# Loads of units 8 to 11 on GpSimd's queue, unit 11 finished by itself, and a new static order

## The chip, the cores and the metric

The kernel runs on one core of one Trainium2 chip. The metric is device time in microseconds (us) of one execution, median of the runs shown. The engines are TensorE (PE, with its weight loads PEld), VectorE (DVE), ScalarE (ACT), GpSimd (POOL) and SyncE (SP). SP does no arithmetic here; it issues DMAs, and so does POOL.

## The reference, cut to what matters

```python
# q, k, v: (8, 8, 576, 64) float32: batch, head, position, head_dim
scores = q @ k.transpose(0, 1, 3, 2) / sqrt(64)
gamma = 1 - 2.0 ** (-5 - arange(8))                  # one per head
D = where(i >= j, gamma ** (i - j), 0)               # i, j: positions
x = ((scores * D) @ v).transpose(0, 2, 1, 3).reshape(4608, 512)
h = x @ w_in                                         # (512, 2048)
g = maximum(0.01 * h, h)
out = g @ w_out                                      # (4608, 512) float32
```

This is a retention layer (causal, with a decay per head and no softmax) and behind it a feed-forward layer with a leaky ReLU.

## The kernel before

**Units.** The 4608 tokens are 36 units of 128 tokens (two chunks of 64), and 9 groups of 512 tokens (four units each). Jobs are named in the code after what they do, and this text uses those names; `u` is a unit, `g` a group.

**Retention, one unit at a time.** `ld{u}.{1,0,2}` loads k, q and v of a unit in float32 (L504; three DMAs, six where the unit spans two batches). `ck{u}` casts k to float16 on ACT (L528), `cq{u}` and `cv{u}` multiply q and v by decay tables (L531, L534; from unit 8 on they are POOL's). `tr{u}` transposes q and k by a DMA that SP issues (L544); units 0 to 7 are transposed on TensorE instead (`tp`, L560, copied out by `yt`, L565). `sa` and `sb` are 16 small matmuls each: the scores of the two chunks (L590) and the new states, k times v (L599). `mk{u}` masks the scores (L605, DVE), `st{u}.{j}` carries the running state from chunk to chunk (L656 to L661, DVE), `sx{u}` casts the states to float16 (L675 or L678, POOL or ACT by the planner's choice). Then the outputs: masked scores times v, and states times q (L697). `x{u}` copies them to the tile xT, the input of the feed-forward layer (L748).

From unit 9 on these matmuls come in bursts: `bu{u}` does, in one job, the rest of the outputs of unit u-2, the first part of the outputs of unit u-1, and `sa` and `sb` of unit u. All bursts share one PSUM tile for outputs (`shared`). A last job `oz` finishes units 34 and 35. So the outputs of unit 11 are complete after bu13.

**Feed-forward.** `h{g}.{f0}.{t0}` are plain blocks of the first product (L822): in groups 0 and 1 four 128-row blocks of w_in for 128 tokens (16 matmuls of 128 columns), from group 2 on one block for 512 tokens (four matmuls of 512 columns). From group 2 on half of the first product is done in two sets of seven smaller products (Strassen's scheme with Winograd's sums): `s{g}.{i}.{1..7}`, four matmuls of 256 columns each (L907), with sums of inputs `xs` (L884) and of weights `ws` (L864), and additions on DVE (L930). `l...` applies the leaky ReLU (L828, L942, ACT). The second product is a set of seven for each group: `p{g}.{1..7}`, 16 matmuls of 256 columns each (L1078), with sums `m{g}` on DVE (L1052), of weights `wm` (L1014), with copies and additions `k1`, `u2`, `v` (L1092, L1094; `k11` is the copy for group 1) and outputs `y` (L1112, L1114). `so{g}.{a}` stores half a group (L1025, SP).

**Weights.** `wi0` to `wi3` load w_in, `wo0` to `wo3` load w_out, both on POOL's queue (L796, L803). Idle stretches of TensorE at the start are filled with matmuls on zeros (`fill`, L1173).

**What sets the order.** The kernel is written out by a planner. Every job gets an engine (or a choice of engines), a cost, the jobs that it comes after, the buffers it opens and uses, and a due time. `Plan.order` plays the jobs through once with those costs and takes at each step the job that can begin first, the more urgent one among those within `slack`; the instructions are then issued in that order, each engine's in its own queue, in order. So costs, due times, the assumed time from a transfer's end to its landing (`land`), safety margins (`SAFE`) and the seed of a small random shift of due times all act on one thing, the order (and the choice of engine where there is one). Loads on POOL's queue follow the string `order` in CFG, where a number is a unit; units beyond its last number are SP's. `aheads` says after which unit's loads each transpose may stand on SP's queue. `gate='wo3'` holds SP's first steady job until the last part of w_out has landed. Loaded tiles have five buffers for each of q, k and v, transposed and cast tiles four.

```python
for u in range(8, NU + 9):
    for j in [loaded[u, x] for x in (1, 0, 2)] if u < NU else []:
        if j.eng == "SP":
            steady(j)
    while to_turn and to_turn[0] + (CFG["aheads"] + (CFG["ahead"],) * NU)[to_turn[0] - 8] <= u:
        steady(turned[to_turn.pop(0), 0])
```

Of the kernel before, what the change touches and what calls it, by code (L numbers as in the profile page):

```python
# [10 lines left out]
FP = mybir.dt.float32  # L11
# [36 lines left out]
class Plan:  # L48
# [62 lines left out]
    @staticmethod  # L111
    def land(eng, t):

        if eng == "SP":
            return 800
        return 900 + min(max(0, t - 5000) * 0.13, 2000) if t < 26000 else 1200
# [169 lines left out]

def _cfg(order="1 wi0 wi1 2 3 wi2 wi3 4 5 6 7 wo0 wo1 wo2 wo3", gate="wo1", nsets=2, at=(4, 9, 14, 99), mk=(), st="POOL", **kw):
    nset = {g: nsets for g in range(2, 9)}
# [8 lines left out]
    for g in range(2, 9):  # L297
        n = nset[g]
        rest = [f for f in blocks if not any(f % 8 in (2 * i, 2 * i + 1) for i in range(n))]
        items = [("b", f) for f in rest]  # L300
        for i in range(n):
            items.insert(min(len(items), at[i]), ("s", i))
        main += [("s" if n else "b", g, items if n else rest), ("L2", g, None)]
# [12 lines left out]
    c = dict(  # L316
        sets=sorted(g for g in nset if nset[g]), set_ids=range(max(nset.values())), ws="POOL/DVE", xs="POOL/DVE",
        ws_due=60000, l1="1627534", one=("a", "b"),
        gate=gate, aheads=(), mask16=bool(mk), ld=5, ap=4, main=main, unit=unit, loads=loads, t0=9000, extra=1300, l_late=1000,
        l2="1265734", l2z="1265734", early=0, margin=60, slack=60, fill_until=60000,  # L320
        split=lambda u: u < 4,
        joined=8, safe=(0, 0), ahead=2, seed=0, noise=0, wm=("DVE/POOL",) * 4, mix=lambda g, n: "DVE", keep="ACT", lead=4500, spread=6500,
    )
# [27 lines left out]
    st='POOL/ACT',  # L351
    aheads=(2, 2, 1, 2, 1, 1, 2),
)
# [3 lines left out]
def kernel(  # L357
# [87 lines left out]
    def half(i):  # L445
# [133 lines left out]
    def inner(u, se, me="DVE"):  # L579
# [37 lines left out]

        if u > J0:
            two = u > J0 + 1

            def burst():
                if two:
                    part_of(u - 2)[1](landed[u - 1])
                part_of(u - 1)[0]()
                sa()
                sb()

            before = outer_needs(u - 1) + ([copied[u - 3]] if u > J0 + 2 else [])
            ja = jb = add(
                f"bu{u}", "PE", (640, 840), burst,  # L630
                [turned[u, 0], turned[u, 1], cast[u, 1], cast[u, 2]] + before, [a, shared],
                [qkT[u], qk16[u], v16[u]] + outer_uses(u - 1) + (outer_uses(u - 2) if two else []), mode="q",
            )
# [12 lines left out]
        for j in range(2):  # L646
# [19 lines left out]
            if scaled and before is not None:  # L666
                c = (c[0] + 400, c[1] + 400)
            after = [jb] + ([before[2]] if before else [])
# [95 lines left out]

    J0 = CFG["joined"]
    shared = Buf(ot_pool, [P, 2, 2, NP, CH], FP, "ot", True, turn=J0)
    parts = {}

    def part_of(u):
        if u not in parts:  # L770
            parts[u] = sums(u, shared, u % 2, u % 2)
        return parts[u]

    def finish():
        u = NU - 1

        def run():
            part_of(u - 1)[1](landed[u])
            part_of(u)[0]()
            part_of(u)[1]()  # L780

        j = add(
            "oz", "PE", (800, 1000), run, outer_needs(u) + [copied[u - 2]], [], [shared] + outer_uses(u) + outer_uses(u - 1), mode="q"
        )
        outer_copy(u - 1, j, shared, (u - 1) % 2, (u - 1) % 2)
        outer_copy(u, j, shared, u % 2, u % 2)
# [393 lines left out]
    for what, g, items in CFG["main"]:  # L1180
# [4 lines left out]
        elif what == "s":  # L1185
            T += sum(865 if kind == "b" else 3600 for kind, f in items)
        else:
# [29 lines left out]
    for u in range(NU):  # L1217
# [7 lines left out]
        if u < J0:  # L1225
            outer(u)
    finish()
    what, n = CFG["gate"]
# [17 lines left out]
    for (what, g, items), t in zip(CFG["main"], starts):  # L1246
# [6 lines left out]
        elif what == "s":  # L1253
            sum_x(g, t)
            at = t
            for kind, f in items:
                if kind == "b":
                    layer1(g, f, 1, 0, TOK, at)
                else:
                    layer1_set(g, f, at)  # L1260
                at += 865 if kind == "b" else 3600
        elif what == "b":
# [52 lines left out]
```

## Time and profile before

| | |
|---|---|
| median of 3 runs | 295.06 us (294.38 to 295.63) |
| the profiled execution | 298.08 us, its span 296.3 us |
| granted TensorE clock | 0.988 of full speed in the mean |
| TensorE busy | 280.9 us (95%) |
| DVE, ACT, POOL busy | 213.6, 155.2, 116.5 us |
| DMA | 50.07 MB; SP's queue 37.76 MB, POOL's 11.54 MB |
| loads issued on POOL | ld0.2 (v of unit 0) and all of units 1 to 9, w_in, w_out |
| loads issued on SP | k and q of unit 0, all of units 10 to 35 |

How to read it: the profile is of one execution, and its times are from the start of the span. Each engine works through its instructions in order; a row's bracket gives the idle time before it and what ended that. "Issue" stands for idle time of an engine that waited for nothing the profile shows. A busy TensorE may still be slower than its peak, so stretches are compared by the starts of jobs. Queue 8 carries TensorE's instructions, 35 transfers of 16 KB. Landings of DMAs are taken from the trace's records.

### The profile page before, as it was taken

The page shows a single profiled execution, that of the slowest core. Times are in us where ns is not written, and L with a number is a line of the kernel's source. Part 1 is how long each engine was busy: PE and PEld are TensorE (multiplying, and loading weights), DVE is VectorE, ACT ScalarE, POOL GpSimd, SP SyncE. Part 2 cuts the span into 40 slices and gives each one's busy share as a digit, 9 for nine tenths or more (in the row PEclk, how much of TensorE's full clock was granted, in tenths as well). Part 3 has the DMA queues.
Part 4 walks back from the last instruction along what each step waited for, and adds up shares of the span by engine and source line. Part 5 has one row for each costly group of instructions (what it writes and reads, how often), then busy time and mean ns, then how long its engine had stood idle before and what let it go on. Part 6 is the DMA issues. An engine that isn't in the chain of part 4 may idle for free.

```text
span 296.3 us, 10315 instructions
## 1 busy us (share of the span) xinstructions
PE 280.9 (95%) x4478; PEld 219.8 (74%) x4478; DVE 213.6 (72%) x366; ACT 155.2 (52%) x281; POOL 116.5 (39%) x128
## 2 busy tenths in 40 slices
PE   7989987999999979999999999999999999999994
PEld 3567986888787657867886787678767876786683
DVE  2568574976898578867985897599668876845662
ACT  2576763735334853278338724783486157705710
POOL 8859683803625435743333324335433211000000
PEclk9999998899999997999999999999999999999999
DMA  7999999399999999989989977999996130003003
GB/s 154 286 246 155 290 216 335 90 195 208 230 223 183 234 214 249 213 236 189 187 155 246 168 160 188 215 181 153 270 144 69 38 145 2 2 0 145 0 2 142
DMA packets 125006, 50.07 MB, mean 169 GB/s; under 512 B 114080, under 2 KB 118816, under 8 KB 124960
## 3 DMA queue, kind: packets, MB, share of 16 engines
q1 hardware_dynamic: 118096, 37.76, 62.5%
q0 software_dynamic: 6576, 11.54, 16.8%
q8 instruction: 35, 0.57, 0.9%
q10 hardware_dynamic: 288, 0.11, 0.1%
q14 instruction: 11, 0.09, 0.1%
HBM read 36.81 MB, written 9.44 MB: 156 GB/s over the span
## 4 chain that ended last, share of the span: by engine, by line
PE 77%; DMA 9%; DVE 5%; issue 4%; POOL 2%; SPq 2%; ACT 0%; DVEq 0%; POOLq 0%
PE acc L1078 33%; PE acc L822 23%; PE acc L907 13%; DMA w_in<-in_moe_w_in_dram 5%; PE ot L697 4%; DMA t<-in_q_dram 3%; PE sc L599 2%; PE sc L590 1%; SPq L544 1%; DVE mix L1052 1%; POOL st L675 1%; POOL qk L531 1%; PE acc L560 1%; DVE s L605 1%; DVE v L534 0%
## 5 line engine op out<-in xcount | busy, mean ns | idle before, releaser
L822 PE MATMUL acc<-xT,w_in 128*128 128x128 f16 (+1 forms) x736 | 89.6, 270 | 2.5 <-issue 2.0
L1078 PEld LDWEIGHTS <-gt 128*128 128x128 f16 x720 | 70.5, 99 | 12.2 <-issue 1.7
L828 ACT ACTIVATE gt<-acc 128x512 f16<-128x512 f32 x88 | 51.9, 595 | 34.0 <-PE acc L822 33.2
L822 PEld LDWEIGHTS <-w_in 128*128 128x128 f16 x736 | 51.8, 99 | 19.1 <-issue 3.2
L531 POOL TENSOR_TENSOR qk<-t,cs 128x512 f16<-128x512 f32 x29 | 32.3, 1114 | 58.6 <-DMA t<-in_q_dram 26.1
L1078 PE MATMUL acc<-w_out,gt 128*128 128x256 f16 x432 | 53.8, 280 | 1.4 <-ACT k L1092 1.3
L748 ACT CAST xT<-ot 128x512 f16<-128x512 f32 x35 | 20.4, 586 | 31.8 <-PE ot L697 31.8
L534 POOL TENSOR_TENSOR v<-t,cs 128x512 f16<-128x512 f32 x29 | 33.3, 1149 | 6.4 <-DMA t<-in_v_dram 3.7
L1078 PE MATMUL acc<-w_mix,gt 128*128 128x256 f16 x288 | 34.4, 273 | 0.0
L1078 PEld LDWEIGHTS <-mix 128*128 128x128 f16 x288 | 28.0, 98 | 3.3
L528 ACT CAST qk<-t 128x512 f16<-128x512 f32 x36 | 22.4, 621 | 9.9 <-DMA t<-in_k_dram 9.8
L942 ACT ACTIVATE gt<-sy 128x512 f16<-128x512 f32 x42 | 25.8, 627 | 2.9 <-DVE sy L930 2.2
L907 PEld LDWEIGHTS <-w_in 128*128 128x128 f16 x224 | 21.6, 98 | 7.3
L605 DVE TENSOR_TENSOR s<-sc,cs 128x512 f16<-128x512 f32 x36 | 24.5, 682 | 1.9 <-PE sc L590 1.7
L930 DVE TENSOR_TENSOR sa<-acc,sk 128x512 f32<-128x512 f32 x14 | 9.7, 691 | 18.0 <-PE acc L907 17.5
L907 PEld LDWEIGHTS <-ws 128*128 128x128 f16 x168 | 15.8, 98 | 7.0
L930 DVE TENSOR_TENSOR sy<-acc,sa 128x512 f32<-128x512 f32 x28 | 18.8, 685 | 2.5 <-PE acc L907 1.8
L697 PE MATMUL ot<-qkT,st 64*64 64x64 f16 x512 | 17.0, 198 | 3.3 <-POOL st L675 2.3
L658 DVE TENSOR_TENSOR s<-sc,s 128x256 f32<-128x256 f32 x40 | 16.7, 416 | 3.6 <-PE sc L590 2.2
L697 PEld LDWEIGHTS <-st 64*64 64x64 f16 x512 | 11.4, 107 | 10.5 <-issue 7.5
L1114 DVE TENSOR_TENSOR osb<-acc,u 128x512 f32<-128x512 f32 (+1 forms) x19 | 12.5, 660 | 8.4 <-PE acc L1078 8.4
L1052 DVE TENSOR_TENSOR mix<-gt 128x1024 f16<-128x1024 f16 x18 | 14.2, 819 | 4.6 <-ACT gt L942 4.0
(65 smaller groups left out, 411.6 us busy)
## 6 DMA issues: line engine op xcount, KB each, us to landing
out_dram<-osb SPq DMA_DIRECT2D x17, 512.0 KB, 4.0
t<-in_k_dram SPq DMA_DIRECT2D x24, 256.0 KB, 4.0
t<-in_q_dram SPq DMA_DIRECT2D x24, 256.0 KB, 4.2
t<-in_v_dram SPq DMA_DIRECT2D x23, 256.0 KB, 4.3
t<-in_v_dram POOLq DMA_DIRECT2D x9, 256.0 KB, 7.7
w_in<-in_moe_w_in_dram POOLq DMA_DIRECT2D x8, 256.0 KB, 7.2
t<-in_k_dram POOLq DMA_DIRECT2D x8, 256.0 KB, 8.2
t<-in_q_dram POOLq DMA_DIRECT2D x8, 256.0 KB, 8.2
```

Source lines behind the costliest of these rows:

```text
L528: copies[e](out=t[:, 1], in_=t32[u, 1][:])
L531: engine[e].tensor_tensor(out=t[:, 0], in0=t32[u, 0][:], in1=decay(u, 0), op=MUL)
L534: engine[e].tensor_tensor(out=s[:], in0=t32[u, 2][:], in1=decay(u, 1), op=MUL)
L605: landed[u] = nc.vector.tensor_tensor(out=s[:], in0=a[:, :, 0], in1=mask_sb.unsqueeze(1).unsqueeze(1).to_broadcast([P, 2, NP, CH]), op=MUL,)
L697: i = nc.tensor.matmul(out=o[half(oo), j ^ swap, slot, c, :], lhsT=lhsT, rhs=rhs, start=(j, oo) not in seen, stop=True, skip_group_check=True,
L748: copies[e](out=x_of(u).rearrange("q c (j t) -> q c j t", j=2), in_=i.rearrange("q j c t -> q c j t"))
L822: nc.tensor.matmul(out=a[:, n, :], lhsT=w_in16[:, c, (f0 + n) * P : (f0 + n + 1) * P], rhs=x[:, c, t0 : t0 + nt], start=(c == 0), stop=(c ...
L828: nc.scalar.activation(out=y[:, f0 : f0 + nf, t0 : t0 + nt], in_=a[:], func=mybir.ActivationFunctionType.Lrelu)
L907: nc.tensor.matmul(out=o[:, m, :], lhsT=lhs[:, c, m * P : (m + 1) * P], rhs=rhs[:, c, :], start=fresh and m == 0 and c == 0, stop=c == 1, ...
L930: nc.vector.tensor_tensor(out=z[:], in0=o[:], in1=keeps[to][:], op=ADD)
L942: nc.scalar.activation(out=y[:, f0 : f0 + 2, half_], in_=z[:], func=mybir.ActivationFunctionType.Lrelu)
L1078: nc.tensor.matmul(out=r[:, tb, :], lhsT=lhs()[:, f, tb * P : (tb + 1) * P], rhs=rhs[:, f, :], start=fresh and i == 0, stop=f == HF - 1, s ...
```

## The change

1. **Loads.** Units 10 and 11 go from SP's queue to POOL's, and the order on POOL's queue is written anew: the loads of unit 1 before wi0, unit 5 before wi3, unit 7 before wo2 and wo3. SP has no load between unit 0's and unit 12's; its first steady job, held by the gate, is now tr8.
2. **Unit 11.** The units from 8 on are split in two segments, 8 to 11 and 12 to 35, each with an output tile of its own in turn. A new job `oz11` finishes the outputs of units 10 and 11 together, after p1.7 in the new order; bu12 holds only `sa` and `sb`. `oz` becomes `oz35`.
3. **The planner's picture.** The assumed landing on SP's queue is 1500 ns after the transfer instead of 800, the safety margin behind a transfer 2000 instead of 1000; several costs, due times, `aheads` and the seed differ. Code for half-width blocks (`halves`) is added and not used.

The order that results has, around what the text speaks of:

```
PE before   ... p0.7 bu9 p0.3 p0.4 bu10 p1.1 p1.2 bu11 p1.6 p1.5 bu12 p1.7 p1.3 bu13 p1.4 s2.0.1 ...
            ... s2.1.5 bu15 s2.1.4 h2.7.0 s2.1.3 h2.15.0 p2.1 bu16 p2.2 p2.6 p2.5 p2.7 bu17 p2.3 p2.4 s3.0.1 ...
PE after    ... p0.7 sa8 p0.3 bu9 p0.4 p1.1 bu10 p1.2 p1.6 bu11 p1.5 p1.7 oz11 p1.3 bu12 p1.4 s2.0.1 ...
            ... s2.1.4 s2.1.3 bu14 p2.1 bu15 p2.2 p2.6 bu16 p2.5 p2.7 bu17 p2.3 p2.4 s3.0.1 bu18 ...
POOL before ... ld8 ld9 cq8 cq9 cv8 cq10 cv9 cv10 sx8 cq11 ... cq18 sx15 cv18 ...
POOL after  ... ld8 ld9.1 cq7 cv7 ld9.0 ld9.2 ld10 ld11 cq8 cq9 cv8 cq10 cv9 sx8 cv10 cq11 ... cv22 cq23 sx20 ...
SP before   ld0 ld10 tr8 ld11 tr9 tr10 ld12 ld13 tr11 so0.0 tr12 so0.1 ld14 tr13 ld15 ld16 tr14 ...
SP after    ld0 tr8 tr9 tr10 ld12 tr11 ld13.1 ld13.0 so0.0 so0.1 ld13.2 tr12 ld14 ld15 ld16 tr13 ...
```

The core of the diff:

```diff
         if eng == "SP":
-            return 800
+            return 1500
...
+    ends = sorted(closes) + [35]
+    segs = tuple(zip([joined] + [z + 1 for z in ends[:-1]], ends))
...
 CFG = _cfg(
-    lead=6000,
-    spread=7000,
-    at=(2, 7, 9, 14),
-    l1='1672534',
+    lead=12000,
+    spread=7500,
+    at=(2, 8, 9, 10),
+    l1='1627543',
...
-    slack=60,
-    l_late=500,
-    extra=800,
-    t0=9000,
+    slack=30,
+    l_late=1000,
+    extra=1600,
+    t0=5000,
...
-    seed=211,
+    seed=296,
...
-    safe=(150, 1000),
-    order='wi0 1 2 wi1 3 4 wi2 wi3 5 wo0 6 wo1 wo2 wo3 7 8 9',
+    safe=(150, 2000),
+    order='1 wi0 2 wi1 3 4 wi2 5 wi3 wo0 6 wo1 7 wo2 wo3 8 9 10 11',
...
-    aheads=(2, 2, 1, 2, 1, 1, 2),
+    aheads=(2, 2, 1, 1, 1, 3, 3),
+    lead2=2000,
+    spread2=7000,
+    closes=(11,),
...
-        "f16": dict(ACT=(505, 640), DVE=(370, 460)),
+        "f16": dict(ACT=(490, 640), DVE=(340, 440)),
...
-        "mul": dict(DVE=(620, 740), POOL=(1010, 1090)),
-        "mix": dict(DVE=(700, 860), POOL=(2050, 2150)),
-        "sum": dict(DVE=(370, 470), POOL=(1010, 1100)),
+        "mul": dict(DVE=(605, 740), POOL=(1010, 1090)),
+        "mix": dict(DVE=(610, 780), POOL=(2050, 2150)),
+        "sum": dict(DVE=(340, 450), POOL=(1110, 1200)),
...
-        if u > J0:
-            two = u > J0 + 1
+        first = first_of.get(u)
+        if first is not None and (u > first or first > J0):
+            one, two = u > first, u > first + 1
+            shared = shares[first]

             def burst():
                 if two:
                     part_of(u - 2)[1](landed[u - 1])
-                part_of(u - 1)[0]()
+                if one:
+                    part_of(u - 1)[0]()
                 sa()
                 sb()
...
-    def finish():
-        u = NU - 1
+    def finish(u):
+
+        f = last_of[u]
+        shared = shares[f]
...
     def x_due(u):
-        return first[u // 4] - CFG["lead"] - CFG["spread"] * (3 - u % 4) if u >= 8 else 1e9
+        if u < 8:
+            return 1e9
+        lead, spread = CFG["lead2" if u < 12 else "lead"], CFG["spread2" if u < 12 else "spread"]
+        return first[u // 4] - lead - spread * (3 - u % 4)
...
-    finish()
+        if u in last_of:
+            finish(u)
```

More of the change, by code (lines that the diff above doesn't have):

```diff
@@ L284, in order, with _cfg @@
         return out
-def _cfg(order="1 wi0 wi1 2 3 wi2 wi3 4 5 6 7 wo0 wo1 wo2 wo3", gate="wo1", nsets=2, at=(4, 9, 14, 99), mk=(), st="POOL", **kw):
+def _cfg(order="1 wi0 wi1 2 3 wi2 wi3 4 5 6 7 wo0 wo1 wo2 wo3", gate="wo1", nsets=2, at=(4, 9, 14, 99), mk=(), closes=(11,), joined=8, halves=(), at2=(8, 9, 10, 11), st="POOL", **kw):
     nset = {g: nsets for g in range(2, 9)}
@@ L321, in _cfg @@
         split=lambda u: u < 4,
-        joined=8, safe=(0, 0), ahead=2, seed=0, noise=0, wm=("DVE/POOL",) * 4, mix=lambda g, n: "DVE", keep="ACT", lead=4500, spread=6500,
+        safe=(0, 0), ahead=2, seed=0, noise=0, wm=("DVE/POOL",) * 4, mix=lambda g, n: "DVE", keep="ACT", lead=4500, spread=6500, lead2=6000, spread2=6000,
     )
@@ L623, in burst @@
                     part_of(u - 2)[1](landed[u - 1])
[L624 to L628 removed]
+                if one:
+                    part_of(u - 1)[0]()
+                sa()
+                sb()
+            before = outer_needs(u - 1) if one else []
+            if u > first + 2:
+                before.append(copied[u - 3])
             ja = jb = add(
[L630 to L632 removed]
+                f"bu{u}", "PE", (640, 840) if one else (290, 490), burst,
+                [turned[u, 0], turned[u, 1], cast[u, 1], cast[u, 2]] + before, [a] + ([shared] if one else []),
+                [qkT[u], qk16[u], v16[u]] + (outer_uses(u - 1) if one else []) + (outer_uses(u - 2) if two else []), mode="q",
             )
@@ L763, in outer @@
         outer_copy(u, j, o)
-    J0 = CFG["joined"]
-    shared = Buf(ot_pool, [P, 2, 2, NP, CH], FP, "ot", True, turn=J0)
+    J0 = CFG["segs"][0][0]
+    shares = {f: Buf(ot_pool, [P, 2, 2, NP, CH], FP, "ot", True, turn=J0 + i) for i, (f, _) in enumerate(CFG["segs"])}
+    first_of = {u: f for f, z in CFG["segs"] for u in range(f, z + 1)}
+    last_of = {z: f for f, z in CFG["segs"]}
     parts = {}
@@ L1185 @@
         elif what == "s":
-            T += sum(865 if kind == "b" else 3600 for kind, f in items)
+            T += sum({"b": 865, "h": 890, "s": 3600}[kind] for kind, f in items)
         else:
```

20 lines of the change are left out of this document (14 added, 6 removed).

## The prediction

> **What bounds the kernel now.** The page first: engine shares, and the slices (40 of 7.4 us).
>
> ```profile
> PE 280.9 (95%) x4478; PEld 219.8 (74%) x4478; DVE 213.6 (72%) x366; ACT 155.2 (52%) x281; POOL 116.5 (39%) x128
> ...
> PE   7989987999999979999999999999999999999994
> ...
> PEclk9999998899999997999999999999999999999999
> DMA  7999999399999999989989977999996130003003
> ```
>
> TensorE is the bound: only 15.4 us of the span are not busy, and two slices lie at a lower clock. The chain of waits, in order of time, says from where on nothing can be won (start, length, what):
>
> ```profile
> 139.54 1.75 PE acc L1078 x16
> ...
> 167.94 1.75 PE acc L1078 x16
> ...
> 196.38 1.75 PE acc L1078 x16
> ...
> 224.79 1.75 PE acc L1078 x16
> ```
>
> These are the first products p3.1, p4.1, p5.1 and p6.1. They stand 28.40, 28.44 and 28.41 us apart, all work of TensorE. So a gain must come before 125 us. The timeline around the largest gap there (start, length, engine, line, operation; the bracket is idle time and what ended it):
>
> ```profile
> 109.15 1.39 POOL L531 TENSOR_TENSOR qk<-t,cs 128x512 f16<-128x512 f32 x1 [4.99 <-DMA t<-in_q_dram]
> 110.50 1.07 POOL L675 CAST st<-s 128x512 f16<-128x512 f32 x1
> 111.62 0.26 PE L697 MATMUL ot<-qkT,st 64*64 64x64 f16 x2 [2.31 <-POOL st L675]
> 112.30 3.16 PE L1078 MATMUL acc<-w_out,gt 128*128 128x256 f16 x16
> 115.29 1.91 PE L1078 MATMUL acc<-w_mix,mix 128*128 128x256 f16 x16
> ```
>
> POOL's cq18 waits for unit 18's q to land, and sx15 is queued behind it. Burst bu16 needs sx15, so TensorE idles 2.31 us, and the next product takes 3.16 us where one takes 1.91. Two earlier gaps, and two windows of 2 us (length; busy time of PE, PEld, DVE, ACT, POOL; clock, DMA share, GB/s):
>
> ```profile
> 48.91 0.40 PE L822 MATMUL acc<-xT,w_in 128*128 128x128 f16 x4 [1.77 <-issue]
> 78.86 1.91 PE L1078 MATMUL acc<-w_out,gt 128*128 128x256 f16 x16 [0.67 <-ACT k L1092]
> 50.00:52.00 2.00, 2.00 (x20) 1.89 (x19) 1.90 (x3) 0.18 (x1) 1.04 (x1) 0.50 1.16 340
> 112.00:114.00 2.00, 2.00 (x34) 1.45 (x26) 2.00 (x4) 1.10 (x2) 1.73 (x2) 0.50 1.24 256
> ```
>
> The clock was 0.5 from 50.02 to 53.43 and from 111.46 to 114.87, 3.41 us each, both times after an idle of about 2 us; 0.82 us of idle at 41.2 did not bring it. A gap of 2 us therefore costs up to 1.7 us more. Last, SP's queue:
>
> ```profile
> SPq L504 <- DMA w_out<-in_moe_w_out_dram: 43.9, 1, 43.9
> SPq L544 <- PE ot L697: 34.5, 16, 6.1
> SPq L544 <- ACT qk L528: 6.4, 1, 6.4
> ```
>
> SP waits for the last of w_out, until 45.8; tr8 then waits 6.4 us for ACT's ck8.
>
> **The change, step by step.** I compare each job's start with the next one's in the trace of before. A product is 1.75 us, a set product (s) 0.44, a 512-column block (h) 0.87, a 128-column group of four blocks 0.89, a burst 0.7.
>
> *Six loads to POOL's queue.* They are ld10 and ld11, three each. Each issue costs POOL 0.87 to 0.93 us, 5.4 in all, beside DMA work: an issue there starts about 0.5 us after the landing of the eighth before it (ld9.0 at 46.22, after wo3's landing at 45.67). So POOL is held until ld11.2 is issued, near 52. Landings on that queue stand 0.75 us apart (ld8: 49.21, 49.93, 50.69). By that and the new order I put ld7's last at 43 (before 48.7), wo3 at 48 (45.7), ld10 at 55 (55.6), ld11 at 57 (64.8). cq8 moves from 50.1 to 52.5; tr8 to tr10 do not wait for that, but for ck8 to ck10. These now stand in ACT's order behind the leaks of h1.12.256, h1.0.384 and h1.8.384, so that the transposes go out near 59, 62 and 64; behind tr8 SP holds tr9, tr10 and ld12, nothing older. ld12 follows at about 65; before it was 65.33. The early loads are thus hidden by ACT's and TensorE's order: worth 0. If ck8 to ck10 ran early, up to 3 us of transfers would be won, not of TensorE. On SP, ld13.2 and tr12 also stand behind so0.1 (output of p0.4), so ld14.1 comes near 79 (78.06 before); bu12 is due nine jobs later, 5 us of slack.
>
> The Trainium skill (DMA: Bandwidth & Descriptors, Issuing engines are not separate DMA queues) says that the issuing engine matters only for issue time. The rows differ: 0.75 us between landings on POOL's queue against 0.9 to 1.0 on SP's (ld19: 112.15, 113.04, 114.05); by the page the six loads save nothing, by the rows 1.2 us of transfer, and neither reaches the sum.
>
> *Start, to the end of h1.12.384.* wi0 now follows ld1. The same bytes precede wi1 (19.08), so h0.0.384 starts near 27.4 (26.94). From there to p0.2 the new order has 31.0 us of matmul time. For the same work (h1.0.384 to h1.12.384 counted in) the trace shows 36.0: lost were waits marked "issue" of 0.45, 0.82 and 1.77, the half clock, about 1.7, and a wait for cv7 of 0.6. Instruction transfers (queue 8, 16 KB, 128 matmuls each) came 6.2 to 6.9 us apart while DMA was full: 27.14, 33.32, 39.67, 46.57, 52.71. The waits fall on matmuls 476, 731 and 858, 128 apart or a multiple. In the new order those numbers fall in the same jobs (h0.8.0, oa5, h1.8.128), so the waits stay. The next one, 986, now comes after only 4.4 us of matmuls (10 us before), with DMA full until 57: a wait of up to 1.8, or none if the clock is halved in it. That stands against cv7's 0.6, which goes (cq7 and cv7, 1.1 each, are now POOL's at 43 to 45). I take +0.4 for the start and nothing else; bounds are -3.0 (the waits go) and +3.5 (1.8 and a second half clock).
>
> *p1.1 to p1.2.* bu10 now stands between, 0.68 us, which covers k11's copy: -0.8 (job lost 0.84 against a product). bu13's 0.14: -0.1.
>
> *Unit 11 finished alone (oz11).* The matmuls are those that bu12 and bu13 did; added are one drain and one change of kind, 0.09 by the bursts' neighbours: +0.1, bounds 0 and 0.4. x11 no longer needs unit 13. bu13 leaves the path to s2.0.1 and comes mid-group. oz11 waits for sx11, with p1.3 queued behind it: bu11, st11.0, mk11, st11.1, sx11 take 2.4 us, p1.5 and p1.7 before it 3.6. On ACT ck13 is ahead of sx11; ld13.1 should be in by 77, oz11 comes near 85.
>
> *bu15, bu16, p2.2.* Removed: 0.55, 2.74 and 1.24, that is -4.5. sx14 to sx16 are now ACT's, where no cq is ahead of them.
>
> *What is late next.* bu14 and bu15 have only p2.1 between them, 1.84 us. From bu14 to bu15 runs st14.0, mk14, st14.1, sx14: 0.42 + 0.68 + 0.42 + 0.62 and about 0.3 of hand-over, 2.4: +0.6 (0 to 1.3). bu16 needs sx15, whose st15.0 stands in DVE's order behind four mixes, 0.7 each alone but 1.09 to 1.54 beside POOL (108.95 to 113.56 in the trace): +0.7 (0, or 2.5 and 1.7 of half clock). From bu16 to bu21 the new order has 25.7 us of matmuls, 5.1 a unit; before, from ld13.2 (75.79) to ld21.2 (123.47) with SP issuing nearly throughout, a unit took 5.96 us. Starting about 2 us ahead, the last transposes come late: +1.0 (0 to 3). Four more set sums (xs) go to POOL, 1.16 us against 0.48 to 0.64: covered by the 8.8 us from bu21 to s4.0.1 and its like, 0 (0.7 each without it). Later landings and new costs act through the order alone.
>
> Sum: 0.4 - 0.8 - 0.1 + 0.1 - 4.5 + 0.6 + 0.7 + 1.0 = -2.6. The profiled execution took 298.08 (span 296.3), so it would take 295.5. The median of the runs is 3.0 lower; I carry the difference over: 295.06 - 2.6 = 292.5. Part of those 3.0 us may be waits that a run without profile lacks.
>
> **The rivals.**
> *POOL's queue once more (slower).* sx20, which bu21 needs, stands behind cv22 and cq23, and cq23 waits for ld23.0. That landed at 135.71; then 1.1 + 0.6 give 137.4, and bu21 is due near 138.5. From one microsecond of lateness on, it decides. Three us late: idle of 2, half clock 1.7, and the same shape at bu25 (sx24 behind cq28), say another 1.5: 5.2 - 2.6 = +2.6, 297.7. For it: it is what happened at bu16, and 5.1 is less than 5.96. Against: from 133 on SP stood idle 1 to 3 us a unit (133.76 to 135.67, 146.05 to 149.46).
> *The instruction waits grow.* A second half clock and the 1.8 us at matmul 986, with p0.6 then behind wm1 on DVE: +3.1, so 295.6. For: DMA stays full until 57. Against: only wider gaps than 0.82 brought it.
> *They go.* -2.6 - 2.5 = 290.0, if denser transfers from POOL leave the instruction queue room. Against: while DMA was full they kept 6.2 to 6.9 us.
> *The half clock comes back anyway.* If the idle before 111.46 did not cause it, the 1.24 at p2.2 returns elsewhere: -2.6 + 1.2 = -1.4, 293.7. For: nothing but that 3.41 us is more than the idle of 2.31. Against: both stretches of 0.5 follow the two longest gaps after the start. The Trainium skill (TensorE: Matmul & The Clock Gate, Part 1) has the clock fall after an idle window of about 3.4 us, which no gap here reaches; the rows differ from it.
>
> **Numbers.** A measurement tells 0.5% (1.5 us) from no change. Forecast 0.45, waits that go 0.12: both faster. Grown waits or small delays 0.17, a half clock that returns 0.03: both same. POOL's queue 0.23: slower. The range 289.5 to 297.2 takes in the bounds above but for some 0.15.
>
> **What would show it.** Right: no idle at bu16, p2.2 at 1.9, s3.0.1 near 121.5 (124.81), groups 28.4 apart, SP's first transpose near 59. Wrong: a transpose before 55, idle over 1 us at bu15 or bu21, or a clock of 0.5 after 60.

## The result, and the profile after

The changed kernel takes 305.67 us (median of 6 runs, 302.23 to 308.58) against 295.54 us (6 runs) of the kernel before beside it: a ratio of 1.031, interval 1.024 to 1.038. The forecast was 292.5 us with a range to 297.2: the wrong side. Its profiled execution took 305.99 us, span 304.2. Ratios here leave out executions more than 1.5% above the fastest of the same kernel; for two kernels below, whose times scatter by 10 us, the range of all executions is given too.

The page of the changed kernel, engine shares and slices (7.6 us each):

```profile
PE 280.9 (92%) x4480; PEld 218.4 (72%) x4480; DVE 223.6 (74%) x362; ACT 152.5 (50%) x279; POOL 130.9 (43%) x140
...
PE   7799996999899989988899979997999899999994
...
PEclk9999999999999999999999998999999999999999
```

TensorE's busy time is the same to a tenth; DVE has 10.0 us more, POOL 14.4 us more. The soft slices have moved: before, they lay in the first 125 us; now most of those behind the start lie in the middle. The starts of jobs say the same (us, and the difference):

| job | before | after | after - before |
|---|---|---|---|
| h0.0.384 | 26.94 | 26.98 | 0.0 |
| s2.0.1 | 91.88 | 90.08 | -1.8 |
| p2.1 | 107.01 | 104.56 | -2.5 |
| s3.0.1 | 124.81 | 120.94 | -3.9 |
| p3.1 | 139.37 | 137.99 | -1.4 |
| p4.1 | 167.78 | 168.02 | +0.2 |
| p5.1 | 196.22 | 201.02 | +4.8 |
| p6.1 | 224.63 | 232.13 | +7.5 |
| p7.1 | 253.87 | 261.94 | +8.1 |
| p8.1 | 279.13 | 287.19 | +8.1 |

To s3.0.1 the forecast (121.5) was met as a sum, though not term by term (see below). From there to p8.1, the stretch in which the prediction saw nothing to win or lose, 154.3 us became 166.2.

First the places that the prediction looked at. The timeline around bu16 (start, length, engine, line, operation; the bracket is idle time and what ended it), two windows (length; busy time of PE, PEld, DVE, ACT, POOL; clock, DMA share, GB/s), and SP's waits (total, times, longest):

```profile
107.30 1.92 PE L1098 MATMUL acc<-w_out,gt 128*128 128x256 f16 x16
...
110.26 1.92 PE L1098 MATMUL acc<-w_mix,mix 128*128 128x256 f16 x16 [1.04 <-DVE mix L1072]
111.97 0.62 ACT L690 CAST st<-s 128x512 f16<-128x512 f32 x1 [2.13 <-DVE s L673]
```

```profile
112.00:114.00 2.00, 1.92 (x74) 1.58 (x73) 2.00 (x5) 1.66 (x3) 0.62 (x1) 1.00 1.11 213
182.00:184.00 2.00, 2.00 (x11) 1.45 (x10) 0.69 (x1) 0.00 (x0) 0.00 (x0) 0.50 0.00 0
```

```profile
SPq L554 <- ACT qk L538: 25.1, 2, 23.9
```

As forecast, sx15 is ACT's, bu16 loses only 0.3 us, p2.2 takes 1.92 where it took 3.16, and the window from 112 to 114 is at full clock (so is 50 to 52). p2.6 behind it waits 1.04 us for a mix. SP issues its first transpose at 57.4; it waited up to 23.9 us for a cast of ACT. The clock of 0.50 is now at 182.

Now the middle. The timeline of the changed kernel in the second product of group 4, and one line of its waits (total, times, longest):

```profile
169.36 1.31 DVE L1072 TENSOR_TENSOR mix<-gt 128x1024 f16<-128x1024 f16 x2
...
171.12 2.73 POOL L904 TENSOR_TENSOR xs<-xT 128x512 f16<-128x512 f16 x2 [1.59 <-ACT xT L763]
172.76 3.19 DVE L1072 TENSOR_TENSOR gt<-gt 128x1024 f16<-128x1024 f16 x2
...
173.81 1.59 POOL L904 TENSOR_TENSOR xs<-xT,xs 128x512 f16<-128x512 f16 x1
...
179.78 0.68 DVE L1114 TENSOR_TENSOR v<-acc,u 128x512 f32<-128x512 f32 x1
180.51 1.84 PE L1098 MATMUL acc<-w_out,gt 128*128 128x256 f16 x12 [2.21 <-DVE v L1114]
```

```profile
PE acc L1098 <- DVE v L1114: 5.7, 3, 2.5
```

Two mixes by themselves take 1.31 us, beside POOL's sums xs 3.19. The second and third of POOL's sums take 1.6 instead of 1.16. DVE is behind, so u4 and v4 come late, and p4.3, which adds to the bank that v4 reads, waits 2.2 us; the half clock follows, 1.7 us more. Groups 3 and 5 have the same wait. The losses from s3.0.1 to p8.1, job by job, sum to 11.8 us, nearly all of the 11.9 by which that stretch grew; some 1 us of them is bu20's wait for its transpose, which is not this. The same place in the kernel before, where the sums come behind v:

```profile
172.75 1.71 DVE L1052 TENSOR_TENSOR gt<-gt 128x1024 f16<-128x1024 f16 x2
...
178.12 1.92 PE L1078 MATMUL acc<-w_out,gt 128*128 128x256 f16 x16
178.72 1.16 POOL L884 TENSOR_TENSOR xs<-xT 128x512 f16<-128x512 f16 x1 [5.41 <-ACT xT L748]
```

The sums are there because the copies x of units 12 and on are due earlier in the new plan (`lead` 12000 instead of 6000): POOL has xs while DVE mixes. The kernel before gives POOL 8 of the sums, all after v of the group; the changed one 12, 11 of them beside the mixes of groups 3 to 6. Those 32 mixes sum to 24.0 us before and 34.3 after. The planner did not see this coming. It lets no two jobs of DVE and POOL run at once that it marks `port`, as it does these sums and mixes, and its own play-through gives the stretch from s3.0.1 to p8.1 155.0 us before and 154.9 after. In that play xs5.0 begins 5.2 us after p4.1, behind the mixes m4.2; in the trace it begins 3.1 us after p4.1 and ahead of them.

### The profile page after: what moved, and what is told of

The parts are those of the page before. It is cut to its first block, busy times and chain, and to the rows that moved or that the text cites. A ratio compares the mean times of both kernels' runs of the same rounds, so it can differ in the third digit from the quotient of the medians.

```text
span 304.2 us, 10285 instructions
## 1 busy us (share of the span) xinstructions
PE 280.9 (92%) x4480; PEld 218.4 (72%) x4480; DVE 223.6 (74%) x362; ACT 152.5 (50%) x279; POOL 130.9 (43%) x140
## 5 line engine op out<-in xcount | busy, mean ns | idle before, releaser
L842 PE MATMUL acc<-xT,w_in 128*128 128x128 f16 (+1 forms) x736 | 87.0, 268 | 2.5 <-issue 2.3
L842 PEld LDWEIGHTS <-w_in 128*128 128x128 f16 x736 | 50.7, 98 | 20.5 <-issue 3.0
L1098 PE MATMUL acc<-w_out,gt 128*128 128x256 f16 x432 | 52.4, 275 | 6.9 <-DVE v L1114 5.7
L544 POOL TENSOR_TENSOR v<-t,cs 128x512 f16<-128x512 f32 x29 | 34.3, 1181 | 8.4 <-DMA t<-in_v_dram 4.4
L1098 PE MATMUL acc<-w_mix,gt 128*128 128x256 f16 x288 | 35.3, 277 | 0.0
L927 PEld LDWEIGHTS <-w_in 128*128 128x128 f16 x224 | 20.9, 98 | 7.5
L690 ACT CAST st<-s 128x512 f16<-128x512 f32 x12 | 7.4, 618 | 26.5 <-DVE s L673 20.1
L1098 PE MATMUL acc<-w_mix,mix 128*128 128x256 f16 x144 | 17.2, 273 | 2.4 <-DVE mix L1072 2.4
```

The costliest lines, as they stand in the source:

```text
L544: engine[e].tensor_tensor(out=s[:], in0=t32[u, 2][:], in1=decay(u, 1), op=MUL)
L842: nc.tensor.matmul(out=a[:, n, :], lhsT=w_in16[:, c, (f0 + n) * P : (f0 + n + 1) * P], rhs=x[:, c, t0 : t0 + nt], start=(c == 0), stop=(c ...
L927: nc.tensor.matmul(out=o[:, m, :], lhsT=lhs[:, c, m * P : (m + 1) * P], rhs=rhs[:, c, :], start=fresh and m == 0 and c == 0, stop=c == 1, ...
L1098: nc.tensor.matmul(out=r[:, tb, :], lhsT=lhs()[:, f, tb * P : (tb + 1) * P], rhs=rhs[:, f, :], start=fresh and i == 0, stop=f == HF - 1, s ...
```

## The experiments

Theory A: the loss is this contention of POOL and DVE. Rival B: it comes from another part of the change (transfers, unit 11, the order), and slow mixes only go along. Each row is measured against the kernel before on the same chip; "mixes" is the sum over groups 3 to 6, "tail" the time from s3.0.1 to p8.1, both of one profiled execution.

| kernel | median (runs) | ratio (interval) | mixes | tail |
|---|---|---|---|---|
| before | 295.54 (6) | 1 | 24.0 | 154.3 |
| after | 305.67 (6) | 1.031 (1.024 to 1.038) | 34.3 | 166.2 |
| e1, after, 11 sums to DVE | 301.63 (4) | 1.021 (1.014 to 1.027) | 26.9 | 161.4 |
| e2, after, sums later in the list | 307.15 (4) | 1.038 (1.032 to 1.044) | 35.7 | 166.2 |
| e3, before, sx15 to ACT | 296.07 (12) | 1.001 (0.997 to 1.005) | 23.5 | 154.3 |
| e4, e3 and bu10 later | 297.90 (11) | 1.007 (1.003 to 1.011) | 24.1 | 155.2 |
| e5, after, due times of before | 298.41 (6) | 1.014 (1.006 to 1.022) | 26.0 | 158.6 |
| e6, before, due times of after | 303.35 (4) | 1.031 (1.022 to 1.039) | 34.1 | 159.4 |
| e7, before, 12 sums added | 298.24 (4) | 1.013 (1.002 to 1.023) | 31.7 | 158.5 |
| e8, after, xs planned for DVE | 300.56 (4) | 1.021 (1.009 to 1.033) | 28.2 | 159.4 |
| e9, before, loads of after | 303.15 (12: 296.4 to 306.2) | 1.008 (1.003 to 1.014) | 24.3 | 154.3 |
| e10, before, unit 11 alone | 296.44 (12) | 1.000 (0.996 to 1.004) | 23.6 | 154.3 |
| e11, before, three named parts | 300.45 (12: 292.5 to 306.9) | 0.995 (0.989 to 1.002) | 25.4 | 154.6 |
| e12, e5 and loads of before | 296.47 (13) | 1.007 (1.004 to 1.011) | 25.5 (e17) | 157.1 (e17) |
| e15, e11 and x7 to ACT | 295.46 (12: 294.0 to 296.8) | 0.998 (0.995 to 1.002) | 24.7 | 156.2 |
| e16, e15 and sx15 to ACT | 295.46 (12) | 1.000 (0.997 to 1.004) | 24.7 | 155.3 |

The kernel before scatters too: its medians beside these rows are 296.8 us (e1 to e4), 296.1 (e5 to e8), 296.5 (e9 to e11), 294.8 (e12) and 296.5 (e15, e16). By the medians of all executions the changed kernel is 3.4% above it, e1 1.6%, e5 0.8%, e6 2.5%, e7 0.7%, e8 1.5%, e9 2.3%, e11 1.3% and e12 0.6%. So a single ratio is good to about one point.

### The sums on DVE (e1)

```diff
+    for j in jobs:                        # after the order is made
+        if j.name in ("xs4.0", "xs4.2", "xs5.0", "xs5.1", "xs5.2", ..., "xs7.2"):
+            j.eng = "DVE"
```

> The changed kernel, its order kept; the eleven input sums xs of groups 4 to 7 that the planner gave to POOL run on DVE at the same place in the order. Theory A (POOL's sums run beside DVE's mixes in the second products and slow both, the mixes from 0.68 to 1.6 us, so u and v come late and p.3 waits): mixes of groups 3 to 6 back to 0.7, the waits at p3.3, p4.3 and p5.3 (1.1, 2.4, 2.7 us) and the half clock at 181 gone, about 296 to 299 us. Theory B (DVE's own order, a burst's sums ahead of u and v, makes v late, POOL is innocent): DVE gets 11 x 0.42 us more ahead of v, so 305 to 308. Theory C (units come too late because transfers take 5.96 us a unit): no change at p.3, 305.

301.63 us, about 4 us less than the changed kernel, but more than the 296 to 299 that theory A expected. Group 5 in the timeline of this run:

```profile
203.26 1.28 DVE L1072 TENSOR_TENSOR gt<-gt,mix 128x1024 f16<-128x1024 f16 x2
...
208.24 1.91 PE L1098 MATMUL acc<-w_out,gt 128*128 128x256 f16 x16
```

The same place in the changed kernel:

```profile
204.57 3.20 DVE L1072 TENSOR_TENSOR gt<-gt 128x1024 f16<-128x1024 f16 x2
...
213.29 0.92 PE L1098 MATMUL acc<-w_out,gt 128*128 128x256 f16 x7 [2.54 <-DVE v L1114]
```

The wait for v5, 2.5 us, is gone, and so is the half clock of group 4. What is left, 1.1 to 1.6 us each behind bu20, p3.7, p4.2 and p4.7, lies in groups 3 and 4, where mixes of 1.2 to 1.5 us still stand beside POOL's casts of loads (bu20, though, waits for its transpose). So A is shown for 3 to 5 of the 10 us (1.0 point by the ratios, 1.8 by the medians, 4.8 us of the tail); the rest was open.

### The sums later in the list (e2): a miss

```diff
+    for g in (4, 5, 6, 7):                # put(names, behind) moves jobs in the list
+        put([f"xs{g}.{n}" for n in ((0, 2) if g == 4 else (0, 1, 2))], f"v{g - 1}")
+        put([f"xs{g}.{n}" for n in ((1, 3) if g == 4 else (3,))], f"y{g - 1}.10.0")
```

> The changed kernel; the same sums stay on POOL but stand in the order behind v of the second products (and the last sum behind y.10), so that they run after the mixes. Theory A: mixes of groups 3 to 6 mostly 0.7, p3.3 to p5.3 wait less than 0.5 us; the first set products of groups 5 to 7 may wait up to 1 us for the sums; 297 to 300 us. Theory B: as the changed kernel, 305. Theory C: 305.

The edit did not do what it says. It moves the jobs in the list, but POOL's own queue stayed the same but for one cast (cv23, now ahead of two sums of group 4), and nothing in it waits for v: the sums of groups 5 to 7 began as long after their p.1 as in the changed kernel (mixes of 1.63 again). The run repeats the changed kernel and tells nothing of A.

### sx15 by itself, and bu10 (e3, e4)

```diff
+    for j in jobs:
+        if j.name == "sx15":
+            j.eng = "ACT"
+    # e4 also moves bu10 from ahead of p1.1 to behind it
```

> The kernel before, with one cast, sx15, on ACT instead of POOL; order kept. If bu16's idle time there is only sx15 queued behind cq18 on POOL: no idle at bu16 (2.7 us lost), no half clock after it (1.2 us), 291 to 292 us. If the units' transfers hold bu16 (tr16 landed at 110.6, 1.0 us before bu16 went on): bu16 waits 1.5 us all the same, 293.5 to 295.

> As the run before it, and bu10 stands between p1.1 and p1.2 instead of ahead of p1.1, which is what the changed order does there. k11's copy is then covered by 0.68 us of burst: 0.6 to 0.8 us less than the run before it, 290.3 to 291.5 us. If the copy does not bound (another wait takes its place): the same as the run before it.

The timeline of e3 at bu16:

```profile
108.52 0.61 ACT L675 CAST st<-s 128x512 f16<-128x512 f32 x1
108.53 1.91 PE L1078 MATMUL acc<-w_out,gt 128*128 128x256 f16 x16
...
112.86 1.91 PE L1078 MATMUL acc<-w_mix,mix 128*128 128x256 f16 x16
```

sx15 is ready in time and the half clock at p2.2 is gone; but the times are those of before, 1.001 (0.997 to 1.005): between 0.8 us gained and 1.4 lost, not 4. So the 4.0 us at bu16 belong to some executions, the profiled one among them, and not to all. Two other kernels with the order of before at this place show both cases: e10 lost 2.63 and 1.35 there, e7 0.95 and nothing. e4 is slower by 2 us: bu10, bu15 and bu16 then lose 0.9 us each in its profile, the last two waiting for their transposes; that it is the later burst that delays these is not shown. Both runs missed what was expected of them (291 to 292 and 290.3 to 291.5).

### The due times alone, undone and done (e5, e6)

```diff
-    lead=12000,                           # e5, on the changed kernel
-    spread=7500,
+    lead=6000,
+    spread=7000,
```
```diff
     def x_due(u):                         # e6, on the kernel before
+        if u >= 12:
+            return first[u // 4] - 12000 - 7500 * (3 - u % 4)
```

> The changed kernel with the two due times of the x copies (lead, spread) set back to those of before (6000, 7000 instead of 12000, 7500); everything else of the change stays, and the order is planned anew. In this order the sums xs of groups 4 to 7 stand at the fourth and fifth last place of the second product again (behind p3.3, p4.3, p5.5, p6.3), not behind p3.6, p4.6, p5.6, p6.6. Theory A (the loss is POOL's sums and casts beside DVE's mixes, brought there by the earlier copies): the mixes of groups 3 to 6 sum to 6 to 6.5 us each (7.4, 9.2, 9.2, 8.6 in the changed kernel), no loss of more than 1 us at p4.7 and p5.7, first products about 28.4 us apart, time 292 to 296: 292 if the 4 us at bu16 count in the times, 295 to 296 if they do not, as the move of sx15 alone said. Rival B (the loss comes with other parts: the order of loads and transposes, unit 11 finished alone, later landings): products stay 29 us or more apart whatever the mixes do, 301 to 306.

> The kernel before with one part of the change alone: the copies x of units 12 and on are due as in the changed kernel (lead 12000, spread 7500), order planned anew; loads, set ends and costs as before. In this order 19 sums xs are POOL's (8 before), those of groups 4 to 7 behind p3.2, p4.6, p5.2, p6.2. Theory A: mixes of groups 3 to 6 sum to 7.5 to 9.5 us, losses of 1 to 2.7 us at the product ahead of p.3 in three or four groups, 301 to 306. Rival B: within 1% of before, 294 to 298.

In e6 one part of the change, put into the kernel before, gives the changed kernel's ratio, 1.031, and its mixes (34.1 us). Group 4 in its timeline:

```profile
175.04 1.40 POOL L884 TENSOR_TENSOR xs<-xT 128x512 f16<-128x512 f16 x1 [2.96 <-ACT xT L748]
175.35 3.09 DVE L1052 TENSOR_TENSOR gt<-gt 128x1024 f16<-128x1024 f16 x2
...
183.34 1.91 PE L1078 MATMUL acc<-w_out,gt 128*128 128x256 f16 x16 [1.05 <-DVE v L1094]
```

But the tail of e6 is only 5.1 us longer, of the changed kernel's 11.9, and group 4 alone has a wait of over 1 us at p.3, where three or four groups were expected. The other 2 us by the medians come before s3.0.1 (125.16; 122.38 in e3, which has no wait at bu16), and the longest wait there, 1.96 us at h0.8.0, is marked "issue" and has nothing to do with the sums. So the earlier due times alone cost most of what the whole change costs, but not all of it in the same places.

e5 is the way back: with everything else of the change kept, the sums stand behind v again, no product waits for v, and 1.7 points of the 3.1 go (2.6 of 3.4 by the medians). It stays above the 292 to 296 that theory A expected, and below rival B. Of the tail's 11.9 us, 4.3 are left: 3.0 of them in group 3 (s3.0.6 waits for xs3, p3.6 for mixes beside casts). The parts do not add up exactly, since every order is planned anew.

### The cost by itself (e7)

```diff
+            for i in range(3):            # behind m{g}.1.1, g = 3 to 6; nobody reads z
+                nc.gpsimd.tensor_tensor(out=z, in0=s[:, 1, 4:6], in1=s[:, 1, 6:8], op=SUB)
```

> The kernel before, order kept, with added work only: in groups 3 to 6 POOL makes three more sums of 128x512 each (into a tile that nobody reads), behind the second of the mixes m.1, so that they lie beside the mixes m.2 and m.3. Nothing else is moved. It measures the disputed cost by itself. Theory A: each sum takes about 1.6 us and the mixes beside it 1.5 instead of 0.7; mixes of a group sum to 7.5 to 9 us, and TensorE waits 1 to 2.5 us a group at the product ahead of p.3: 299 to 304. Rival C (the slower mixes are hidden where the burst stands later, so it is the place of bursts and copies that costs): mixes slow down but 295 to 297. If POOL's sums run late behind a cast that waits for a load, the mixes stay at 0.7 and the run tells nothing.

Lines of group 5, and of bu16, where this kernel still has the instructions of before:

```profile
198.17 3.95 POOL L1286 TENSOR_TENSOR zz<-mix 128x512 f16<-128x512 f16 x3 [4.89 <-DVE mix L1052]
...
199.80 2.87 DVE L1052 TENSOR_TENSOR gt<-gt 128x1024 f16<-128x1024 f16 x2
...
206.22 1.03 PE L1078 MATMUL acc<-w_out,gt 128*128 128x256 f16 x8 [1.44 <-DVE v L1094]
```

```profile
108.48 0.25 PE L697 MATMUL ot<-qkT,st 64*64 64x64 f16 x4 [0.54 <-POOL st L675]
```

Twelve sums that nobody needs lengthen the mixes by 7.6 us and the tail by 4.2; the time grows by 1.3%, 3.7 us (interval 0.2 to 2.3%; 2.2 us by the medians). That is some 0.2 to 0.3 us a sum, on TensorE's path, with no order changed. It is less than the 299 us at least that was expected. Only group 5 has a wait for v (1.61 us); in the other groups p.3 comes late enough for v. Why the same slowing of the mixes costs more in the changed kernel is not shown by itself; there, three groups have that wait.

### The sums planned for DVE (e8)

```diff
+    xs="DVE",                             # on the changed kernel
```

> The changed kernel with DVE alone allowed for the sums xs, known to the order (11 moved sums, as in the first run on this, but the order takes account of them). Theory A: mixes stand beside POOL only where it casts loads (0.7 to 1.5 us each), time like the first run's 301.6 or a few us below, 297 to 302. Rival B: 303 to 306.

Like e1, and within what was expected: with no sum on POOL, one to two mixes of 1.53 us remain in every group.

### The other parts of the change, one by one (e9, e10, e11)

```diff
-    order='wi0 1 2 wi1 3 4 wi2 wi3 5 wo0 6 wo1 wo2 wo3 7 8 9',        # e9 and e11
-    aheads=(2, 2, 1, 2, 1, 1, 2),
+    order='1 wi0 2 wi1 3 4 wi2 5 wi3 wo0 6 wo1 7 wo2 wo3 8 9 10 11',
+    aheads=(2, 2, 1, 1, 1, 3, 3),
+    closes=(11,),                                                     # e10 and e11
-            return 800                                                # e11
+            return 1500
```

> The kernel before with one part of the change alone: units 10 and 11 are loaded by POOL's queue, the order of weights and units and the lead of the transposes are the change's; landings, costs, due times, seed and unit 11's finish are as before. Planned anew; from p2.1 on TensorE's order is that of before, and POOL's sums xs stand where they stood. The prediction's own step: the early loads are worth 0, the front moves by -3.0 to +3.5, nothing comes after 125 us: 293 to 298. Rival B (this part carries what is left of the loss, 298.4 against 296.1 in the kernel with the early due times alone undone): 298 to 301. If it is faster by 1 to 3 us, the front of the changed kernel was a gain that the rest covered up.

> The kernel before with one part of the change alone: unit 11's outputs are finished by themselves (oz11, the burst's sums of units 8 to 11 closed there); everything else as before, planned anew; the order is the same but for the stretch from p1.5 to h2.14. The prediction's step: +0.1 (0 to 0.4), so 295 to 297. A rival: oz11 or p1.3 waits for sx11, or bu12 opens late: 297 to 299.

> The kernel before with the three parts that the change names, and nothing else of it: the loads on POOL's queue, unit 11 finished alone, SP's landings assumed 1500 instead of 800 ns. Due times, cost table, seed and slacks are those of before. From p2.1 on TensorE's order is that of before. Theory A (the loss is the earlier due times of the x copies, which bring POOL's sums beside the mixes): no loss from 125 to 279 us, first products 28.4 apart, 292 to 297; it may then be the version that is faster than both. Rival B (the named parts themselves cost): 298 to 302.

Unit 11 by itself costs nothing that can be told. None of the three has a tail of more than 154.6 us in the table: so the named parts are not where the loss in the tail is. But with the loads on POOL's queue the times scatter, e9 from 296 to 306 and e11 from 292.5 to 307, and the medians, 303.15 and 300.45, lie above what was expected (293 to 298, 292 to 297). One more execution of each of these two, profiled (e13, e14):

> The same kernel as the one with the loads alone, one more look. Its times lay between 296.4 and 306.2, in two clumps (296 to 298, 302 to 306). If this execution is of the later clump, the profile shows where 6 us go: by theory D a chain of waits before 125 us (a unit's transpose that comes late because SP's and POOL's queues meet, bu13 to bu17, each followed by a half clock of 3.41 us, 1.7 us); by a rival, a stretch of the first 60 us, where instruction transfers and loads meet. If it is of the first clump it shows bu13's 3.10 us once more and tells nothing new.

> The same kernel as the one with the three named parts, one more look. Its times lay between 292.5 and 306.9. By theory D the difference lies before 125 us, in waits of bursts bu12 to bu17 and half clocks; groups from 125 us on 28.4 apart as before. By the rival it lies in the first 60 us.

They took 303.91 and 303.42 us. The tails are 154.3 and 156.5; most of the time is lost at 55 to 64 us. The timeline of the first:

```profile
53.21 7.29 DVE L1034 TENSOR_TENSOR w_out<-w_out 128x1024 f16<-128x1024 f16 x1
...
58.92 1.03 POOL L541 TENSOR_TENSOR qk<-t,cs 128x512 f16<-128x512 f32 x1
59.92 1.48 POOL L544 TENSOR_TENSOR v<-t,cs 128x512 f16<-128x512 f32 x1
...
61.87 0.68 DVE L763 CAST xT<-ot 128x512 f16<-128x512 f32 x1
...
62.60 0.61 PE L842 MATMUL acc<-xT,w_in 128*128 128x128 f16 x4 [5.28 <-DVE xT L763]
```

One weight difference wm0, 0.68 us by itself, takes 7.29: it ends only when POOL is at the last of seven casts that follow each other without a pause. x7 is queued behind it, and h1.0.384 waits for x7; half clock for 6.8 us follows. In the execution of e11 with a span of 292.4 the two engines took turns instead:

```profile
52.93 1.55 DVE L1034 TENSOR_TENSOR w_out<-w_out 128x1024 f16<-128x1024 f16 x1
...
53.87 1.51 POOL L544 TENSOR_TENSOR v<-t,cs 128x512 f16<-128x512 f32 x1
```

So theory D was wrong in the place (not bu12 to bu17; bu13's wait of 3 us for its transpose is in e9 and e13 alike), its rival right. By the order on POOL's queue, units 10 and 11 are issued before unit 8 is cast, and the casts then follow each other. In the kernel before and in the changed one x7 is ACT's; it became DVE's when e9 and e11 were planned anew. So these two runs changed more than the parts they name, and the wait for x7 is not a cost of the change.

### That wait taken away (e15, e16)

```diff
+        if j.name in ("x7",):             # e16: ("x7", "sx15")
+            j.eng = "ACT"
```

> The kernel before with the three named parts (300.5 alone, between 292.5 and 306.9), order kept, and one edit: the copy x7 is ACT's instead of DVE's. In two executions of the later clump the next block h1.0.384 waited 4.3 and 5.3 us for x7, which stood on DVE behind a weight difference (w_out, 128x1024) that took 7.3 us while POOL cast units 8 to 10 without a pause; a half clock followed each time. In an execution of the earlier clump the same difference took 1.55 us. Theory E (this wait is the scatter): the later clump is gone, 292 to 298 throughout, median 294 to 296, at or a little below before. Rival: the scatter stays, since the late differences hold up p0.6 or the next mixes instead; median 298 to 302.

> The same with sx15 on ACT too (bu16 lost 1.0 to 1.5 us to it in the executions seen). Theory E: 291 to 296, up to 1 us below the one with x7 alone; by the earlier run on sx15 alone no difference that can be told.

e15 settles it. Its profiled execution has the starved difference too, and TensorE does not care:

```profile
53.99 7.28 DVE L1034 TENSOR_TENSOR w_out<-w_out 128x1024 f16<-128x1024 f16 x1
...
58.81 3.74 PE L842 MATMUL acc<-xT,w_in 128*128 128x128 f16 x64
```

All 12 executions lie between 294.0 and 296.8; the clump above 302 is gone. The median is 295.46, ratio 0.998 (0.995 to 1.002): the named parts of the change, mended, are worth nothing that can be told from no change, but these times are steadier than those of the kernel before beside it (293.7 to 301.5 in 23 executions). e16 adds nothing in the median; one of its executions took 302.68, with a wait of 2.9 us behind oa7. No version here is clearly faster than before. In the changed kernel x7 is ACT's already, and its own starved difference (53.21, 5.89 us) costs TensorE nothing there.

### What is left (e12, e17)

```diff
-    lead=12000, spread=7500,              # on the changed kernel
+    lead=6000, spread=7000,
-    order='1 wi0 2 wi1 ... 8 9 10 11', aheads=(2, 2, 1, 1, 1, 3, 3),
+    order='wi0 1 2 wi1 ... 7 8 9', aheads=(2, 2, 1, 2, 1, 1, 2),
-            return 1500
+            return 800
```

> The changed kernel with the early due times undone and the loads too (units 10 and 11 on SP's queue again, order of weights, lead of transposes and assumed landing as before); unit 11's finish, the new costs, seed and slacks stay. TensorE's order in groups 3 and 4 is nearly that of the kernel with the due times alone undone (298.4). Theory A2 (what is left of the loss, 298.4 against 296.1, comes with the loads: units ahead of their transfers, POOL's casts beside the mixes of groups 3 and 4): 294.5 to 296.5, mixes of groups 3 and 4 6.5 us or less. Rival (it comes with the new cost table, seed and slacks): 297.5 to 299.5.

> One more look at the changed kernel with the early due times and the loads undone (296.5), whose first profiled execution ran TensorE at half pace throughout and cannot be read. Theory A2: mixes of groups 3 and 4 take 6.5 us or less and s3.0.1 to s5.0.1 takes 57 to 57.5 us (60.3 in the kernel with the due times alone undone, 56.8 before).

296.47, 1.007 (1.004 to 1.011), against 1.014 with the due times alone undone. The intervals overlap (and the medians give 0.6% and 0.8%), so whether the loads carry half of this rest isn't settled. The execution e17 of the same kernel took 295.03, with mixes of 7.2 and 7.3 us in groups 3 and 4 and 58.1 us from s3.0.1 to s5.0.1, between the two expectations. The last 0.7% then belong to what else is in this kernel: unit 11's finish (0 by e10), cost table, seed, slacks. Which of those is open.

## Why the prediction was wrong

- **The step that failed** is "Four more set sums (xs) go to POOL ... covered by the 8.8 us from bu21 to s4.0.1 and its like, 0 (0.7 each without it)". It priced the sums by their own length and asked only when their results are needed. It did not ask what else runs at that time, nor what they do to it. The rows for it were in the prediction: the mixes "0.7 each alone but 1.09 to 1.54 beside POOL", used for bu16 and not here. By e6 the earlier due times cost 3.1% when put in alone, 9 us (7 by the medians); by e5 undoing them brings back 1.7 points, 5 us (2.6 points by the medians). The sums themselves are a part of that: taking them off POOL (e1) brings back 1.0 to 1.8 points, and as many added for nothing (e7) cost 0.7 to 1.3%. How the rest of what the due times cost divides among casts beside mixes, moved bursts and waits at the front is open.
- **"From where on nothing can be won"** was right and one-sided. TensorE waits for nothing there, so nothing can be won; but DVE's work between u and p.3 has little slack, and 11.8 us were lost in small pieces. What has no waits has no proof of slack either.
- **bu15, bu16 and p2.2, -4.5.** Right for the pair of profiles at bu16 and p2.2. That s3.0.1 came at 120.94, forecast 121.5, is in part luck: to s2.0.1 1.8 us were gained where the terms gave 0.4, and from there 2.1 where they gave 3.2. In the times the waits are mostly not there: e3 takes them away and moves the time by -0.8 to +1.4 us, e7 loses 0.95 at bu16 with the instructions of before. The prediction carried the 3.0 us between its profiled execution and the median over unchanged, though it said that they might be such waits. Without this term its sum is +1.9, 297.0; the kernel with the due times undone (e5) took 298.4. So this term is the second one that failed: it took one execution's waits for the kernel's.
- **Start, +0.4.** From h0.0.384 to p0.2 it took 34.3 us for work that took 36.0: the half clock at 50 did not come, though h1.8.128 lost 1.98 us at 45.4. A bound, not the value, held.
- **k11 by bu10, -0.8.** p1.1 lost nothing, but p1.2 (0.57) and bu11 (1.03) did: nothing won.
- **oz11 +0.1, bu13 -0.1.** oz11 lost nothing; e10 gives 1.000. Right.
- **+0.6, +0.7 and +1.0.** p2.2 and bu16 lost 1.21 and 0.30, and bu20 and bu21 0.96 and 0.53: 1.5 and 1.5. About right in size; the 1.21 was m2.1.0 beside POOL's cast, not sx15.
- **Early loads, 0.** tr8 at 57.4 and no loss: right for this order. That the same loads bring a wait of 4 to 5 us in another order (e13, e14), and none with x7 on ACT (e15), shows that it hung on x7's engine.
- **The rivals.** "POOL's queue once more" had the right sign and engine and the wrong place: bu21 lost 0.53 and bu25 nothing. POOL did not come late; it came early, beside DVE. The returning half clock came, once, behind a wait for v.
- **A reading.** The clock line of the page has three digits below 9 (8, 8 and 7), not two. They are the two stretches at half clock that the prediction then times, so nothing hangs on it.

## What to carry to other kernels

Price a job that moves onto a neighbour engine by what it does to the work beside it, not only by its own length and the date of its result; look in the trace for the longest time of the same instruction, and see what ran beside it. When a plan moves copies earlier, follow what they release. And a wait in a stretch full of transfers may belong to one execution: before it is booked as a gain, profile a second execution, or give it the width of the runs' spread.

## What the runs showed of the hardware

- **DVE and POOL.** A mix or weight difference of 128x1024 takes 0.67 to 0.69 us when it starts while POOL runs nothing, even if POOL starts during it, and mostly up to 1.64 when it starts during one of POOL's sums or multiplications; it then ends about 0.55 us after POOL's does (172.83 after 172.28), and POOL's next sum takes 1.60 instead of 1.16. The Trainium skill (SBUF — State Buffer, SBUF: two separate sides) says that the two engines share a pair of ports under an exclusive lock, held for a whole instruction by whichever starts first. The rows agree. Not expected: against a chain of POOL's instructions DVE can lose every round. The same kind of difference took 1.4 to 1.6 us where the engines took turns, and 5.89, 7.29, 7.31 and 7.28 where they did not; in two executions of one kernel (e11 and e14) it went one way and the other. In the four long cases DVE's instruction began while POOL was issuing a DMA just ahead of its casts; in the two shortest, 1.55 and 1.58 us (e11 and e9), it began during the first cast. But two others, 4.53 and 4.93 us (e5 and e2), began during a cast as well, so what decides is open.
- **The half clock.** Inside the runs it comes in stretches of 3.41 us or a multiple. In the changed kernel it followed an idle of 2.2 us (178.3 to 180.5) and not one of 2.5 us (210.8 to 213.3); the first lies inside one window of the grid that the stretches keep, the second across two. The Trainium skill (TensorE: Matmul & The Clock Gate, Part 1) has a free-running window of that length, and an idle window of it before the clock falls; the grid agrees, the length of idle doesn't. No other length comes out of the traces as a limit: inside one window 1.5 us of idle brought it at 49.39 in e15, and 2.0 did not at 215.46 in e2.
- One execution of e12 took 564.95 us: its products took twice their time throughout, while its profile shows no drop of the clock. The ratio leaves it out; what happened is open.
